# GLA recurrence followed by a multiplicative FFN: from the tenth step on, v's load is SyncE's first transfer of a step

## The chip, the cores and the metric

One core of a Trainium2 chip runs the kernel. Its engines are TensorE (PE in the profile, its weight loads PEld), VectorE (DVE), ScalarE (ACT), GpSimd (POOL) and SyncE (SP). Each works through its own instructions in order; they wait for one another through semaphores. SyncE computes nothing: it issues most of the transfers between HBM and the core's memory, one after another, into one queue that 16 DMA engines serve. The metric is the device time of one execution in microseconds, the median of the runs, lower is better.

## What is computed

The first part is a gated linear recurrence over 768 time steps for 4 batches and 8 heads of 48 values; its output, seen as 3072 tokens of 384 values, goes through a multiplicative FFN:

```python
# q, k, v, alpha: (4, 8, 768, 48), float32
for t in range(S):
    state = alpha[:, :, t, :, None] * state + np.einsum('bhd,bhe->bhde', k[:, :, t], v[:, :, t])
    y[:, :, t] = np.einsum('bhd,bhde->bhe', q[:, :, t], state)
x = y.transpose(0, 2, 1, 3).reshape(3072, 384)
a = x @ w1          # 384 x 1024
b = x @ w2          # 384 x 1024
h = a * b @ w3      # 1024 x 1024
out = h @ w_out     # 1024 x 384
```

The FFN's weights come in as 64-bit floats and are turned into float32 by integer and float operations on the chip.

## The kernel before

**Tiling.** Time is cut into chunks of 128 steps: 6 to a batch, 24 in all (N). A step of the main loop, n = 0 to 24, works on one chunk with all its heads, and on its neighbours, because the work is pipelined over the steps. Three chunks (384 tokens) make a group of the FFN; there are 8 groups. The kernel has two parts. In the first, the recurrence and the conversion of w1 and w2 run, and from step 6 on pieces of the FFN's first products (`gate`) fill TensorE's time. In the second, from about 188 us on, TensorE does the rest of the gates, the folding of w3 and w_out, and the last projection without a pause.

**A step of the first part, for n from 9 on.** In the order of the program:
- SyncE: `store()` writes chunk n-2's output x to the scratch tensor xd (four transfers, L307); in steps 11, 15 and 19 `load_x` reads a whole group of xd back as xT (L542); `load_a(n + 5)` loads alpha, `load_kq(n + 4)` loads k and q (L154, L155), and `load_v(n + 2)` loads v (L160). Transfers of raw weights (L238) and of gate results (`abd`, L631) stand between these blocks, where the program makes them.
- `attention(n)`: TensorE forms the scores of chunk n and, between them, the output of chunk n-1 (`quarters(n - 1)`, L426 and L466), which reads v(n-1) and a copy of it with the halves exchanged, vt. `transposed(n + 1)` turns q and k of the next chunk (L383), and ScalarE copies them out of PSUM (L385).
- `turn_v(n)`: GpSimd makes vt(n) from v(n) (L168, two instructions).
- the output of chunk n-1 is copied by ScalarE (L446); its stores go out in the next step.
- `outer(n)`: TensorE multiplies k and v of chunk n for the state (L395); chunks 11, 17 and 23 end a batch and need none.
- pieces of a gate (L556, nine products each): `exact` takes two PSUM banks. ScalarE moves the first to t (L565), VectorE adds the second to it (L567). Step 14 has two pieces here and one more later.
- `decayed(n + 2)`: VectorE multiplies q and k by the decays (L361). `logs(n + 4)`: ScalarE takes the logarithm of alpha (L326). `decays(n + 3)`: TensorE sums the logarithms over time (L348), ScalarE exponentiates (L351, L352).
- in some steps GpSimd carries the state's decay over a pair of chunks through small transfers: `ends` (L333, L354, L356) out and `dec` (L369) back, then L412 to L414.

**What sets the order.** Every engine's instructions stay close to the order of the program text; some are held behind marks (`tc.issue_after`). SyncE issues in order, too. So a load's place among SyncE's transfers is decided by where its call stands in the loop.

**Buffers.** v has four buffers (`vs`), so v(n+2) overwrites v(n-2). kq has three, alpha two, vt two. PSUM's eight banks are handed out in turn by `bank()`: the ninth request gets the first bank again and waits until that is read. Alpha of chunk n+5 is loaded in step n and read by ScalarE in step n+1; v of chunk n+2 is loaded in step n and used in steps n+2 and n+3; k and q of chunk n+4 are loaded in step n and read in step n+2.

`FIRST` is 6 and `TURNED` is 8.

Of the kernel before, what the change touches and what calls it, by code (L numbers as in the profile page):

```python
# [48 lines left out]
def kernel(  # L49
# [31 lines left out]
    TURNED = 8  # L81
# [30 lines left out]
    def after_marks(*names):  # L112
        stack = ExitStack()
        for x in names:
            stack.enter_context(tc.issue_after(mark[x]))
        return stack
# [15 lines left out]
    def rows(src, n):  # L132
        b, c = divmod(n, NCH)
        return src[b, :, ds(c * C, C), :].rearrange("h p d -> p h d")
# [4 lines left out]
    def load_a(n):  # L139
        if paired(n):  # L140
            if n % 2 == 0:
                b, c = divmod(n, NCH)
                x = pairs[n // 2 % 2]
                nc.sync.dma_start(out=x.rearrange("p h s d -> p h (s d)"), in_=alpha[b, :, ds(c * C, 2 * C), :].rearrange("h (p s) d -> p h (s d)", s=2))
                st["a", n] = st["a", n + 1] = x
        elif n < N:
            st["a", n] = inp.tile([C, H, D], FP32, tag="ac", name="ac", bufs=2)
            nc.sync.dma_start(out=st["a", n], in_=rows(alpha, n))

    def load_kq(n):  # L150
        if n >= N:
            return
        st["kq", n] = inp.tile([C, 2, H, D], FP32, tag="kq", name="kq")
        nc.sync.dma_start(out=st["kq", n][:, 0], in_=rows(k, n))  # L154
        nc.sync.dma_start(out=st["kq", n][:, 1], in_=rows(q, n))  # L155

    def load_v(n):
        if n < N:
            st["v", n] = vs[n % len(vs)]
            (nc.gpsimd if 2 < n < 8 else nc.sync).dma_start(out=st["v", n][:, :, 0:D], in_=rows(v, n))  # L160
# [121 lines left out]
    def fetch(ahead=3):  # L282
        while weights and len(begun) < ahead:
            begun.append(weights.popleft())
            next(begun[-1])
# [17 lines left out]
    def store():  # L303

        while later:
            dst, src = later.popleft()
            nc.sync.dma_start(out=dst, in_=src)  # L307
# [170 lines left out]
    def attention(n):  # L478

        low, high = quarters(n - 1) if turned(n - 1) else ([], [])  # L480
        done = None
        if n < N:
            own, done = quarter_scores(n)
            high = own + high
        low, high, at = deque(low), deque(high), [0, 0]
        while low or high:
            k = 0 if not high or low and at[0] <= at[1] else 1
            cost, f, x = (low, high)[k].popleft()
            at[k] += cost
            f(x)  # L490
        if done:
            done()

    def scores(n):
        qkT = st["qkT", n]
        sc = [bank().rearrange("p (j c) -> p j c", j=NP) for _ in range(2)]
        for j in range(NP):
            for i in range(2):
                r = ds(DP * i, D)
                nc.tensor.matmul(sc[i][:, j, :], qkT[r, 0, j, :], qkT[r, 1, j, :], start=True, stop=True)  # L500
        ms = work.tile([C, 2, NP, C], FP32, tag="ms", name="ms")
        for i in range(2):
            masked = nc.vector.tensor_tensor(ms[:, i].bitcast(I32), sc[i].bitcast(I32), keep_bc, op=ALU.bitwise_and)
        ends_of_part1[0] = mark["ms", n] = masked.ins
        st["ms", n] = ms
# [3 lines left out]
    def attend_state(n):  # L509
        qkT = st.pop(("qkT", n))  # L510

        y = [bank()[:, 0:HP * C].rearrange("p (j c) -> p j c", c=C) for _ in range(2)]
        st["y", n] = y, [(half * HP + j, i, y[i][ds(DP * half, DP), j, :])
                         for j in range(HP) for i in range(2) for half in range(2)]
        if n % NCH:
            for j, i, to in st["y", n][1]:
                r = ds(DP * i, D)
                nc.tensor.matmul(to, Ts[n % 2][r, j, :], qkT[r, 1, j, :],  # L520
                                 start=(j % HP == 0), stop=False, skip_group_check=True)
# [18 lines left out]
    def load_x(g, queue=nc.sync):  # L540
        st["xT", g] = xp.tile([C, KM, TG], FP32, tag="xT", name="xT")
        queue.dma_start(out=st["xT", g], in_=xd[g].rearrange("(k p) t -> p k t", p=C))  # L542
# [82 lines left out]
    def gate(g, f):  # L625
        yield from (late_gate if late else early_gate)(g, f)
# [68 lines left out]
    def run(pieces):  # L695

        for _ in range(pieces):
            if not fill:
                return
            try:  # L700
                next(fill[0])
            except StopIteration:
                fill.popleft()
# [22 lines left out]
    FIRST = 6  # L726
    begin = {FIRST - 3 + 4 * g: (g, range(FH if g < 4 else KF)) for g in range(5)}
    loads = {8: 1, 11: 2, 15: 3, 19: 4}

    for n in range(N + 1):  # L730
        if not 1 < n < FIRST:
            store()
        if n in loads:
            load_x(loads[n])
        if n != 1 and not 2 < n <= FIRST:
            load_a(n + 5)
        raws = (3, 3, 3, 3, 2, 2, 3, 3)[n] if n < 8 else 4
        for m in (n + 3,) * (n <= FIRST) + (n + 4,) * (n >= FIRST):
            load_kq(m)
            if 2 < n <= FIRST and m == n + 3:  # L740
                load_a(n + 5)
            if 1 < n < FIRST:
                store()
            if n < FIRST - 2:
                fetch(raws)
        if n >= FIRST:
            load_v(n + 2)
        if 0 < n <= TURNED:
            attend_state(n - 1)
        if n < TURNED:  # L750
            scores(n)
        else:
            attention(n)
        transposed(n + 1)
        if n == 1:
            decays(3)
            load_a(6)
            with after_marks(("e", 3)):
                logs(4)
        if n == FIRST + 1:  # L760
            run(2)
        if n < FIRST:
            with after_marks("pool"):
                load_v(n + 2)
        if n - 2 in begin and n > FIRST:
            g, tiles = begin[n - 2]
            with after_marks(("ms", n), ("qkT", n + 1)):
                split_x(g, 0)
            fill.extend(gate(g, f) for f in tiles)
        if n == FIRST:  # L770
            with after_marks("l", ("qkT", n + 1)):
                split_x(0, 0)
            fill.extend(gate(0, f) for f in begin[n - 3][1])
        pieces = ((3, 3, 2, 0) if n > FIRST + 3 else (0, 3, 3, 0))[(n - FIRST) % 4] if n >= FIRST else 0
        if n == 0:
            with after_marks(("qkT", 0)):
                logs(2)
            decays(2)
            with after_marks(("e", 2)):
                logs(3)  # L780
        early, ready = n < FIRST, len(thirds) if n > 2 else n // 2
        marks = (*[("qkT", n + 1)] * (n < N - 1), *[("qk", n + 1), ("ms", n)] * early, *["x3"] * (n - 2 in begin and n > FIRST))
        if n < N - 2 and n != FIRST:
            with after_marks(*marks):
                convert(2 if early else 1, raws)
        advance(n)
        turn_v(n)
        if n > TURNED:
            st.pop(("x", n - 1))()
        elif n:  # L790
            attend(n - 1)
        outer(n)
        if n > FIRST:
            third(ready)
        run(pieces > 0)
        if early:
            with after_marks(*marks):
                convert(1, raws)
        with after_marks(*[("ms", n)] * (n < 3)):
            decayed(n + 2)  # L800
        if not early:
            with after_marks(*[("qkT", n + 1)] * (n < N - 4)):
                logs(n + 4)
        if n == 4:
            load_x(0)
        convert(early and n > 0, raws)
        run(pieces > 1)
        if n:
            decays(n + 3)
        if n <= FIRST:  # L810
            third(ready)
        if 0 < n < FIRST:
            with after_marks(("e", n + 3)):
                logs(n + 4)
        if n == FIRST:
            with after_marks("x3", ("e", n + 3)):
                convert(2, raws)
        elif n < N - 2:
            convert(n == FIRST - 1 if early else n % 3 == 0, raws)
        if n == FIRST - 1:  # L820
            assert len(done) == 2 * KM
        run(pieces > 2)
        if n == N - 3:
            while begun:
                convert(1)
            weights.extend(load_out(j) for j in range(KF))
            fetch(4)
# [90 lines left out]
```

## Time and profile before

| | |
|---|---|
| median of 3 runs | 468.36 us (467.34 to 472.93) |
| the profiled execution | 467.49 us, span 465.8 us, mean granted TensorE clock 0.992 |
| TensorE busy | 448.6 us, 96% of the span |
| TensorE weight loads busy | 426.8 us, 92% |
| VectorE, ScalarE, GpSimd busy | 363.3 us (78%), 277.9 us (60%), 96.0 us (21%) |
| transfers | 80.38 MB, mean 173 GB/s; 97904 of 149381 packets under 512 B |
| v, issue to landing | 3.2 to 6.7 us, median 5.1 |
| alpha, issue to landing | 2.4 to 8.1 us, median 4.4 |
| k and q, issue to landing | 3.6 to 7.5 us, median 5.2 |

Of the page's view of 40 slices (11.6 us each), three rows: TensorE's busy tenths, the clock granted to it, and the load of the DMA engines:

```profile
PE   4998999997999999999999999999999999999996
PEclk9999999998899999999999999999999999999999
DMA  9999999987998878578755437412115976555511
```

The first part covers the first 16 slices. TensorE is busy nearly all the time after the first slice, with a dent in the tenth, where the clock is below full as well; the DMA engines are full for most of the first part and have room in the second.

### The profile page before, as it was taken

What the parts mean: (1) busy time and instruction counts of PE and PEld (TensorE: products, weight loads), DVE (VectorE), ACT (ScalarE), POOL (GpSimd) and SP (SyncE); (2) the same over time, 40 slices, a digit from 0 to 9 for tenths busy, and PEclk for the clock granted to TensorE, in tenths of its full rate; (3) what the DMA queues carried; (4) which work ended last, traced back from release to release, by engine and by line L of the source; (5) the groups of instructions that cost most, each with busy time, mean ns of one, the idle gap of its engine ahead of it and who ended that gap; (6) DMA issues with size and microseconds to landing.
All of it is one profiled execution on the core that took longest, in us unless ns stands there. A gap on an engine that the chain in (4) does not pass through costs nothing.

```text
span 465.8 us, 11170 instructions
## 1 busy us (share of the span) xinstructions
PE 448.6 (96%) x4296; PEld 426.8 (92%) x4296; DVE 363.3 (78%) x578; ACT 277.9 (60%) x544; POOL 96.0 (21%) x186
## 2 busy tenths in 40 slices
PE   4998999997999999999999999999999999999996
PEld 2676699986999999999999999999999999999996
DVE  2779995998578969999997899998542967766671
ACT  4685966866468554898765676765544533333330
POOL 6144323215222533022222111211110000000000
PEclk9999999998899999999999999999999999999999
DMA  9999999987998878578755437412115976555511
GB/s 175 257 207 223 269 220 219 225 190 187 184 189 169 181 161 220 178 233 235 212 183 185 132 125 193 146 48 91 51 35 144 243 223 182 184 171 161 168 51 52
DMA packets 149381, 80.38 MB, mean 173 GB/s; under 512 B 97904, under 2 KB 139120, under 8 KB 149328
## 3 DMA queue, kind: packets, MB, share of 16 engines
q1 hardware_dynamic: 143552, 64.44, 57.3%
q0 software_dynamic: 5776, 15.22, 11.1%
q8 instruction: 34, 0.56, 0.6%
q14 instruction: 19, 0.16, 0.1%
HBM read 57.58 MB, written 22.06 MB: 171 GB/s over the span
## 4 chain that ended last, share of the span: by engine, by line
PE 86%; DMA 5%; DVE 3%; ACT 3%; SPq 2%; issue 1%; DVEq 0%; ACTq 0%
PE bank L556 71%; PE bank L426 4%; PE bank L383 2%; PE bank L395 2%; DMA kq<-in_q_dram 2%; PE bank L466 2%; DMA v<-in_v_dram 1%; PE bank L500 1%; PE bank L345 1%; PE bank L342 1%; DMA raw<-in_moe_w_dram 1%; SPq L155 1%; DVE qk L361 1%; PE bank L348 1%; PE bank L526 1%
## 5 line engine op out<-in xcount | busy, mean ns | idle before, releaser
L556 PE MATMUL bank<-x,w 128*128 128x384 f32 x1152 | 211.1, 339 | 0.6 <-DVE ms L473 0.6
L556 PEld LDWEIGHTS bank<-x,w 128*128 128x128 f32 x1152 | 202.3, 189 | 1.9 <-DVE ms L473 1.0
L556 PE MATMUL bank<-w3o,ab 128*128 128x384 f32 x576 | 100.2, 336 | 0.0
L556 PEld LDWEIGHTS bank<-w3o,ab 128*128 128x128 f32 x576 | 99.9, 188 | 0.0
L581 ACT ACTIVATE bank<-bank 128x384 f32<-128x384 f32 x96 | 45.8, 477 | 40.4 <-PE bank L556 40.3
L565 ACT ACTIVATE t<-bank 128x384 f32<-128x384 f32 x64 | 31.6, 495 | 57.6 <-PE bank L556 57.6
L631 POOL DMA_DIRECT2D abd<-ab x45 | 25.8, 573 | 133.9 <-DVE ab L617 115.8
L682 DVE TENSOR_TENSOR ab<-abl,ab 128x1024 fp32r<-128x1024 f32 x24 | 29.4, 1224 | 12.8 <-ACT ab L681 12.7
L681 ACT ACTIVATE ab<-abl 128x1024 fp32r<-128x1024 f32 x24 | 25.5, 1061 | 20.1 <-PE bank L556 18.5
L556 PE MATMUL bank<-wo,w3T 128*128 128x384 f32 x192 | 35.9, 334 | 0.0
L617 DVE TENSOR_TENSOR ab<-bank,r 128x384 f32<-128x384 f32 x44 | 24.3, 552 | 13.6 <-ACT bank L581 7.0
L251 ACT ACTIVATE power<-power,rebias 128x512 uint32<-128x512 uint32 (+1 forms) x36 | 25.2, 701 | 14.1 <-DVE power L250 14.1
L556 PEld LDWEIGHTS bank<-wo,w3T 128*128 128x128 f32 x192 | 33.5, 188 | 0.0
L385 ACT COPY qkT<-bank 128x512 f32<-128x512 f32 x48 | 26.2, 599 | 10.2 <-PE bank L383 10.2
L361 DVE TENSOR_TENSOR qk<-kq,e 128x768 f32<-128x768 f32 x24 | 23.4, 976 | 10.9 <-ACT e L352 8.1
L567 DVE SCALAR_TENSOR_TENSOR o<-bank,t 128x384 f32<-128x384 f32 x24 | 13.4, 557 | 22.4 <-issue 13.7
L567 DVE SCALAR_TENSOR_TENSOR r<-bank,t 128x384 f32<-128x384 f32 x40 | 22.0, 551 | 10.7 <-ACT t L565 5.1
L683 DVE SCALAR_TENSOR_TENSOR ab<-ab,abl 128x1024 fp32r<-128x1024 f32 x24 | 29.2, 1218 | 0.0
L254 DVE SCALAR_TENSOR_TENSOR power<-raw,power 128x512 uint32<-128x512 uint32 (+1 forms) x36 | 23.9, 663 | 4.0 <-ACT power L251 4.0
L253 DVE SCALAR_TENSOR_TENSOR mant<-mant,rest 128x512 f32<-128x512 uint32 (+1 forms) x36 | 23.7, 658 | 2.5 <-ACT rest L246 2.5
L466 PE MATMUL bank<-qkT 48*64 48x128 f32 (+1 forms) x512 | 24.9, 247 | 0.0
L426 PE MATMUL bank<-ms,v 64*64 64x64 f32 (+1 forms) x256 | 24.4, 244 | 0.0
(100 smaller groups left out, 695.6 us busy)
## 6 DMA issues: line engine op xcount, KB each, us to landing
abl<-abd SPq DMA_DIRECT2D x24, 512.0 KB, 4.6
abd<-ab POOLq DMA_DIRECT2D x45, 192.0 KB, 3.0
raw<-in_moe_w_dram SPq DMA_DIRECT2D x64, 128.0 KB, 3.4
raw<-in_moe_w_dram SPq DMA_DIRECT2D x12, 512.0 KB, 5.9
xT<-xd POOLq DMA_DIRECT2D x9, 576.0 KB, 5.0
kq<-in_k_dram SPq DMA_DIRECT2D x24, 192.0 KB, 5.2
kq<-in_q_dram SPq DMA_DIRECT2D x24, 192.0 KB, 5.6
out_dram<-o SPq DMA_DIRECT2D x24, 192.0 KB, 3.5
```

Of the source, the lines that this page charges most:

```text
L361: mark["qk", n] = nc.vector.tensor_mul(qks[n % 3][:, :, :, 0:D], st.pop(("kq", n)), st.pop(("e", n)).rearrange("p i (h d) -> p i h d", h=H ...
L385: mark["qkT", n] = nc.scalar.copy(qkT[:, :, :, ds(DP * half, DP)], tp[half]).ins
L426: nc.tensor.matmul(to, w, x, start=(at, i) not in first, stop=True, skip_group_check=True)
L466: nc.tensor.matmul(sc[1][to, j, :] if late else sc[0][to, :, j, :], qkT[r, 0, j, ds(DP * late, DP)], q, start=True, stop=True)
L556: nc.tensor.matmul(p, w[part][i], x[part][i], start=start and part == parts[0] and i == 0, stop=stop and part == parts[-1] and i == n - 1, ...
L565: nc.scalar.activation(t, p1, AF.Copy, scale=(1.0 + 1.0 / P) * scale)
L567: nc.vector.scalar_tensor_tensor(to, p2, scale, t, op0=ALU.mult, op1=ALU.add)
L581: nc.scalar.activation(p, p, AF.Copy, scale=1.0 + 1.0 / P)
L631: (nc.gpsimd if late else nc.sync).dma_start(out=abd[g][:, f, :], in_=ab)
L681: nc.scalar.activation(t[:, 0], ab, AF.Copy, scale=1.0 - 2.0 ** -13)
L682: nc.vector.tensor_sub(t[:, 1], ab, t[:, 0].bitcast(FP32))
L683: nc.vector.scalar_tensor_tensor(t[:, 2], t[:, 0].bitcast(FP32), -1.0 - 1.0 / P, ab, op0=ALU.mult, op1=ALU.add)
```

## The change

From step 9 on (`n > TURNED`) the call of `load_v(n + 2)` stands at the top of the step, ahead of `store()`, `load_x`, `load_a` and `load_kq`, instead of behind them. For steps 6 to 8 it stays where it was. It concerns the loads of v(11) to v(23), made in steps 9 to 21; later calls do nothing.

```diff
     for n in range(N + 1):
+        if n > TURNED:
+            load_v(n + 2)
         if not 1 < n < FIRST:
             store()
         if n in loads:
...
                 store()
             if n < FIRST - 2:
                 fetch(raws)
-        if n >= FIRST:
+        if FIRST <= n <= TURNED:
             load_v(n + 2)
```

In the built kernel the order of instructions on TensorE, VectorE and ScalarE is the same as before. On SyncE the 13 loads of v stand ahead of their step's stores. On GpSimd two places change, although the text of the program does not: one of the two copies of v(11) (L168) now comes before the small store of alpha's row (L333), and the copies of v(15) come before two small loads (L369).

## Prediction

> **What bounds the kernel now.** The page's chain comes first: who sets the end.
>
> ```profile
> PE 86%; DMA 5%; DVE 3%; ACT 3%; SPq 2%; issue 1%; DVEq 0%; ACTq 0%
> ```
>
> TensorE does, so the change is worth what it adds to or takes from TensorE's idle time and slow time. The change touches steps 9 to 21, so I asked next for TensorE's waits from 56 to 190 us (total, times, longest):
>
> ```profile
> PE bank L395 <- DMA v<-in_v_dram: 3.3, 1, 3.3
> PE bank L556 <- DVE ms L473: 0.6, 1, 0.6
> ```
>
> One wait in the whole stretch is for v. TensorE's timeline shows it (start, time, engine, line, count, idle before); the last three lines are the same work a step later, undisturbed:
>
> ```profile
> 115.01 1.10 PE L395 MATMUL bank<-v,qk 128*64 128x48 f32 x16 [3.33 <-DMA v<-in_v_dram]
> 116.03 5.39 PE L556 MATMUL bank<-x,w 128*128 128x384 f32 x18
> ...
> 125.97 0.67 PE L395 MATMUL bank<-v,qk 128*64 128x48 f32 x16
> 126.57 3.41 PE L556 MATMUL bank<-x,w 128*128 128x384 f32 x18
> 129.81 0.51 PE L348 MATMUL bank<-la,sums 128*128 128x384 f32 x2
> ```
>
> This is outer(14), in step 14: TensorE was ready at 115.01 - 3.33 = 111.68. And what follows the wait is slow: 1.10 us for 0.67, and 5.39 for 3.41. The granted clock (PEclk, ahead of the last two columns) says why:
>
> ```profile
> 113.00:113.50 0.50, 0.00 (x0) 0.00 (x0) 0.50 (x2) 0.50 (x2) 0.10 (x1) 1.00 0.63 230
> 113.50:114.00 0.50, 0.00 (x0) 0.00 (x0) 0.50 (x3) 0.14 (x1) 0.00 (x0) 0.56 0.99 373
> 120.00:120.50 0.50, 0.50 (x3) 0.50 (x3) 0.00 (x0) 0.00 (x0) 0.50 (x1) 0.62 1.29 204
> 120.50:121.00 0.50, 0.50 (x5) 0.50 (x4) 0.00 (x0) 0.07 (x1) 0.50 (x2) 1.00 0.87 206
> ```
>
> It halves at about 113.56 (0.56 over that half microsecond is 0.06 us at full and 0.44 at half), 1.9 us after TensorE stopped, and is full again at about 120.38. Last, SyncE's own order in step 12, which loads v(14), and the next alpha:
>
> ```profile
> 104.28 1.87 SPq L307 DMA_DIRECT2D xd<-x  x4
> 106.25 0.40 SPq L148 DMA_DIRECT2D ac<-in_alpha_dram  x1
> 106.69 0.58 SPq L154 DMA_DIRECT2D kq<-in_k_dram  x1
> 107.32 1.90 SPq L155 DMA_DIRECT2D kq<-in_q_dram  x1
> 109.33 0.81 SPq L160 DMA_DIRECT2D v<-in_v_dram  x1
> ...
> 115.10 0.40 SPq L148 DMA_DIRECT2D ac<-in_alpha_dram  x1
> ```
>
> v(14) is issued last, at 109.33, and lands 5.6 us later, at 114.97.
>
> **Part 1: v goes to the front (13 loads, v(11) to v(23)).** No instruction is added or removed. In step 12 v would be issued where the first store now stands, at 104.28, 5.05 us sooner. The v loads of this profile took 3.2 to 6.7 us to land, median 5.1; so it lands at 107.5 to 111.0, by the median at 109.4, all before 111.68. The wait of 3.33 goes, and with it the slow clock: 1.10 - 0.67 = 0.43 and 5.39 - 3.41 = 1.98. Sum: 5.74 us. Other v loads that are close get slack too: v(18), issued at 139.49, lands 5.3 later at 144.8, and TensorE uses it at 145.41.
>
> Does v wait longer at the front? It overwrites the buffer of v(n-2), whose last readers are GpSimd's copies in step n-2 and the quarters of attention(n-1). The stores behind it send ScalarE's copy of those same quarters, which comes later. So whatever holds v would have held the stores; v(14)'s buffer was last read at 91.3 (the end of attention(11)), 13 us before. I cost this wait at nothing. If the cover were gone, the four stores, alpha, k and q behind v would be held by as much.
>
> **Part 2: what v passes is issued later.** Per step these are four output stores, alpha, k and q, and in steps 11, 15 and 19 the load of xT. Each is later by one issue of v (0.40 to 0.81 us where it isn't held) and at most by one transfer of v: k and q, the same 192 KB, land 0.7 to 1.1 us apart in this stretch. It doesn't add up over the steps, since a step still sends the same bytes: each is one v behind, once. Lower bound: nothing or a gain, because from 103.6 to 107.6 the DMA engines were about half idle (share 0.62, after 1.26 in the 3.6 us before) and v would fill that. Upper bound 0.81 + 1.05 = 1.9 us. I take 0 for alpha(18), nearest to the row where the queue had a hole.
>
> [...]
>
> **Part 3: what is late next.** Alpha. Its lead is a single step, and ScalarE, which works in order, takes its logarithm ahead of clearing the gate's banks:
>
> ```profile
> 118.29 0.52 ACT L326 ACTIVATE la<-ac 128x384 f32<-128x384 f32 x1 [4.64 <-DMA ac<-in_alpha_dram]
> 118.72 0.47 ACT L565 ACTIVATE t<-bank 128x384 f32<-128x384 f32 x1
> 119.39 0.56 DVE L567 SCALAR_TENSOR_TENSOR r<-bank,t 128x384 f32<-128x384 f32 x1 [1.69 <-PE bank L556]
> ```
>
> ScalarE waited 4.64 us for alpha(18) and nobody noticed, since TensorE stood still for v. Without that, TensorE goes from 111.68 through outer(14), 18 + 9 gate products and decays(17). A step later this took 131.81 - 125.97 = 5.84, so attention(15) is due at 117.5. The eight banks go round in turn: step 14 takes 14 (2 sums, 2 scores, 2 transposes, 1 outer, 2 + 2 + 2 for the gate, 1 decays), so attention(15)'s second sum takes the bank that this t clears, and its first score bank the one that this r clears, at 119.39 + 0.56 = 119.95. TensorE then idles from 117.5 to 119.9: 2.4 us come back. With alpha(18) later by 0 to 1.9 this is 2.4 to 4.3; if it landed 2.4 sooner, 0.
>
> Does the clock halve again? In the trace it did after 1.9 us of idle time and didn't after the 0.63 us at 94.56 (clock 1.00 there). 2.4 lies above the first, so I can't exclude it: bounds 0 and the 0.43 + 1.98 = 2.41 us measured; I take a third, 0.8, since this gap is the shorter one. [...]
>
> Alpha(22) is next in line (landed 4.5 us after 144.59, at 149.1; ScalarE waited 0.7 us for it). With TensorE 2.5 us earlier, attention(19), now at 151.3, is due at 148.8, while the second t behind that alpha ends at 149.54 + 0.48 = 150.0: up to 1.2 us come back. But SyncE was held there by the queue (1.19 us at 140.23, 2.96 for four stores at 141.52) behind v(18), which is now gone sooner. I take 0 and keep 1.2 for the range. k and q have over 2 us (k(20) and q(20) landed by 142.8 and are read at 149.48).
>
> GpSimd's queue changes in two places. The copies of v(11) come partly in front of the store of alpha's row (now at 85.86): v(11), at 79.05 instead of 84.83, should land by 84.2. The copies of v(15) come in front of two small loads (now at 120.00): v(15), from 111.38, lands by about 116.5. Nothing, while v is that early.
>
> Sum: -5.74 + 2.4 + 0.8 = -2.5 us. The profiled execution took 467.49 us (span 465.8, 1.7 around it), 0.87 below the median of the runs, 468.36; so 465.0 for it, and 465.9 for the median.
>
> **The rivals.** *Full gain:* alpha(18) lands before 116 too because v left the hole earlier and the queue is shorter, and nothing comes back: 468.36 - 5.74 = 462.6. For it: that half idle stretch. Against: from 107.6 to 115 the share was 0.86, and alpha(18) stays behind as many bytes. *A wait in place of another:* alpha(18) lands about 0.9 later, TensorE stands 3.3 us at attention(15) and the clock halves: 3.3 + 2.4 = 5.7, so 468.4, no change. *Slower:* one mechanism, alpha behind v in the queue at attention(15). From a landing 0.9 us later than now on, the new gap costs more than the old; at the full 1.9 the gap is 4.3 + 2.4 = 6.7, +1.0 net; held once more by a full queue, as SyncE was for 2.54 us at 101.18, the gap is 6.8 + 2.4, +3.5. So 469.4 to 471.9, say 470.7. For it: alpha(17) (issued at 106.25, landed 4.2 later) came just as ScalarE read it, at 110.44, so alpha has no slack here. *The move doesn't happen* is out: the instruction order of the built kernel shows all 13 loads ahead of their stores.
>
> **How the numbers follow.** Partial gain 0.50 (own range 464 to 467.5), full gain 0.18, no change 0.17, slower 0.15. The range 462.2 to 470.6 takes in the first three and half the last. Two per cent, 9.4 us, is about what a measurement of this kernel tells from no change. Faster than 459.0 would need more idle time than steps 9 to 24 hold (5.74 + 0.63): 0.02. Slower than 477.7 needs several new gaps with a halved clock: 0.06. Within: 0.92.
>
> **What would show it.** The 3.33 us wait of L395 for v is gone, and the 18 products behind it take 3.4 us. TensorE has a gap at attention(15) (L426, L466), released by ScalarE's t or VectorE's r behind an alpha; its length against 2.4 us decides between the cases, and the clock rows whether it halved. Wrong if v is still waited for, if SyncE is held at L160 by TensorE or GpSimd, or if step 15 has no gap (full gain).

## The result and the profile after

| | before | after |
|---|---|---|
| median of 22 runs each, on the same chip | 467.32 us (465.31 to 472.93) | 464.66 us (462.91 to 467.82) |
| ratio, 95% interval | | 0.9946 [0.9928, 0.9965] |
| the profiled execution | 467.49 us, span 465.8 us | 467.82 us, span 466.1 us |

The change is worth about 2.5 us (0.54% of 467.3), well inside two per cent. The profiled execution of the changed kernel is the slowest of its 22, slower than the profiled one before: stages have to be compared, not spans. TensorE reached the transposes (L383) of step 9, where the change begins, 1.17 us later than before (80.12 instead of 78.95), although nothing was changed up to there. From there to the transposes of step 22 it took 92.63 us instead of 93.58.

TensorE's waits from 56 to 190 us (total, times, longest), the changed kernel:

```profile
PE bank L466 <- ACT t L565: 2.2, 1, 2.2
PE bank L556 <- DVE ms L473: 0.7, 1, 0.7
```

The wait of L395 for v, 3.3 us, is gone; a wait for ScalarE's t of 2.2 us is there. TensorE's timeline in steps 14 and 15 (start, time, engine, line, count, idle before):

```profile
113.45 0.67 PE L395 MATMUL bank<-v,qk 128*64 128x48 f32 x16
114.05 3.41 PE L556 MATMUL bank<-x,w 128*128 128x384 f32 x18
...
119.30 0.43 PE L426 MATMUL bank<-qkT,T 48*64 48x128 f32 x4
121.96 0.48 PE L466 MATMUL bank<-qkT 48*64 48x128 f32 x2 [2.23 <-ACT t L565]
```

outer(14) goes through at full speed: 0.67 us instead of 1.10, and 3.41 instead of 5.39 for the 18 products behind it. Then attention(15) stops for 2.23 us. What released it, in ScalarE's timeline:

```profile
121.01 0.52 ACT L326 ACTIVATE la<-ac 128x384 f32<-128x384 f32 x1 [5.62 <-DMA ac<-in_alpha_dram]
121.44 0.85 ACT L565 ACTIVATE t<-bank 128x384 f32<-128x384 f32 x2
```

ScalarE stood 5.62 us in front of the logarithm, for alpha(18), and the t that clears a bank of PSUM came behind it. The granted clock (third column from the right) around this gap:

```profile
121.00:121.50 0.50, 0.00 (x0) 0.00 (x0) 0.00 (x0) 0.49 (x2) 0.50 (x2) 1.00 1.11 222
121.50:122.00 0.50, 0.04 (x4) 0.04 (x4) 0.06 (x1) 0.50 (x3) 0.50 (x1) 0.64 0.80 159
...
125.00:125.50 0.50, 0.50 (x18) 0.47 (x10) 0.50 (x2) 0.10 (x1) 0.20 (x1) 0.95 1.19 240
```

It halves at 121.64 and is full again at 125.05, 3.41 us later. Before, the slow stretch was 6.83 us long. Last, SyncE's order in steps 12 and 13:

```profile
106.11 0.38 SPq L160 DMA_DIRECT2D v<-in_v_dram  x1
106.58 2.09 SPq L307 DMA_DIRECT2D xd<-x  x4
108.77 0.40 SPq L148 DMA_DIRECT2D ac<-in_alpha_dram  x1
...
112.83 0.38 SPq L160 DMA_DIRECT2D v<-in_v_dram  x1
113.31 3.33 SPq L307 DMA_DIRECT2D xd<-x  x4
116.75 0.40 SPq L148 DMA_DIRECT2D ac<-in_alpha_dram  x1
```

v(14), issued at 106.11, lands at 109.78, 3.7 us ahead of its use. Alpha(18), in step 13, goes out behind v(15) and four stores that hold SyncE for 3.33 us, and lands at 120.98.

The balance can be checked term by term. From the transposes of step 14 to those of step 15 TensorE took 14.36 us before (110.96 to 125.32) and 12.75 after (112.80 to 125.55): 1.61 less. The terms are -5.74 (the wait and the slow clock at outer(14)), +2.23 (the gap) and +1.97 (attention(15) needed 6.25 - 2.23 = 4.02 us of work to the transposes, where before it needed 125.32 - 123.27 = 2.05), together -1.54.

### The profile page after: what moved, and what is told of

Its sections match the earlier page's. It is cut to its first block, busy times and chain, and to the rows that moved or that the text cites. A ratio compares the mean times of both kernels' runs of the same rounds, so it can differ in the third digit from the quotient of the medians.

```text
span 466.1 us, 11166 instructions
## 1 busy us (share of the span) xinstructions
PE 448.6 (96%) x4296; PEld 425.3 (91%) x4296; DVE 362.8 (78%) x578; ACT 277.4 (60%) x544; POOL 96.0 (21%) x186
## 4 chain that ended last, share of the span: by engine, by line
PE 84%; DMA 6%; DVE 3%; ACT 3%; issue 1%; SPq 1%; DVEq 0%; ACTq 0%
PE bank L556 70%; PE bank L426 4%; DMA kq<-in_q_dram 3%; PE bank L383 2%; PE bank L466 2%; DMA ac<-in_alpha_dram 2%; PE bank L395 1%; DVE qk L361 1%; PE bank L342 1%; PE bank L345 1%; DMA kq<-in_k_dram 1%; PE bank L348 1%; PE bank L500 1%; PE bank L526 1%; DMA abd<-ab 1%
## 5 line engine op out<-in xcount | busy, mean ns | idle before, releaser
L556 PEld LDWEIGHTS bank<-x,w 128*128 128x128 f32 x1152 | 200.1, 188 | 2.8 <-DVE ms L473 1.3
L466 PE MATMUL bank<-qkT 48*64 48x128 f32 (+1 forms) x512 | 26.3, 254 | 2.2 <-ACT t L565 2.2
L466 PEld LDWEIGHTS bank<-qkT 48*64 48x64 f32 x512 | 23.8, 139 | 2.8 <-ACT t L565 2.5
```

The source lines that it names most:

```text
L466: nc.tensor.matmul(sc[1][to, j, :] if late else sc[0][to, :, j, :], qkT[r, 0, j, ds(DP * late, DP)], q, start=True, stop=True)
L556: nc.tensor.matmul(p, w[part][i], x[part][i], start=start and part == parts[0] and i == 0, stop=stop and part == parts[-1] and i == n - 1, ...
```

## The experiments

The time from the transposes of step 9 to those of step 22 is cut at steps 12 and 15. These are the starts of L383 on TensorE in the profiled executions, and the waits are TensorE's in that stretch. "v" are waits for v, "alpha" waits that a late alpha causes through ScalarE (t or e), "q" those through VectorE's decayed q and k (r), "none" idle time without a releaser in the profile, always at attention(10); "slow" counts stretches of 3.41 us at half clock. Waits for VectorE's masked scores (ms, up to 0.78 us in seven of the executions) are left out. Each row is one profiled execution, and the experiments are told below.

| kernel | steps 9 to 12 | 12 to 15 | 15 to 22 | v | alpha | q | none | slow |
|---|---|---|---|---|---|---|---|---|
| before | 21.33 | 25.04 | 47.21 | 3.33 | | | | 2 |
| before, again | 21.95 | 21.28 | 50.02 | 0.67 + 1.89 | 0.52 | | | |
| before, log behind t | 22.01 | 23.69 | 47.80 | 2.83 + 0.52 | | | 0.43 | 1 |
| v(14) alone to the front | 21.36 | 20.17 | 49.54 | 1.52 | | | | |
| all but v(14) to the front | 21.81 | 20.48 | 47.30 | 0.45 | | | 0.89 | |
| after | 22.00 | 23.43 | 47.20 | | 2.23 | | | 1 |
| after, again | 23.70 | 19.30 | 47.26 | | | | 1.33 | 1 |
| alpha ahead of v | 22.12 | 19.48 | 48.95 | | | 1.01 | 1.31 | |
| alpha ahead of v, again | 21.81 | 20.86 | 48.94 | | 0.76 | 1.45 | | |
| stores ahead of v | 21.72 | 23.03 | 49.16 | | 1.23 + 1.58 + 0.93 + 0.53 | | 0.90 | |
| after, log behind t | 22.26 | 19.22 | 47.21 | | | | 1.44 | |
| after, log behind t, again | 23.69 | 19.30 | 48.28 | | 0.52 | | 1.32 | 1 |
| v(14) at the back, log behind t | 21.86 | 20.75 | 47.61 | 1.47 | | | 0.26 | |
| from v(13) on, log behind t | 23.88 | 19.30 | 47.21 | | | | 1.52 | 1 |

**One transfer alone, and all but that one.** The theory was that the wait of outer(14) carries the change. Against the changed kernel:

```diff
-        if n > TURNED:
+        if n == 12:
             load_v(n + 2)
...
-        if FIRST <= n <= TURNED:
+        if n >= FIRST and n != 12:
             load_v(n + 2)
```

> Only v(14) is loaded at the front of its step; the other twelve loads stay behind k and q as before. Theory A (one transfer, v(14), carried the gain): as the whole change, 2.7 us faster than before (ratio 0.992 to 0.997), no wait of L395 for v, and a gap of 1.5 to 2.5 us at attention(15) that ends with ScalarE's t behind alpha(18). Rival B (the gain is spread over thirteen loads and a queue with fewer holes): at most a third of it, ratio 0.998 or more.

465.84 us, ratio 0.9971 [0.9947, 0.9996]: by the medians a little over half of the gain, which neither side had expected (the interval takes in the whole gain and almost none). The wait for v did not vanish but moved on to step 18, where v(18) is still SyncE's last transfer (the waits of TensorE in this kernel, then the instruction that waited):

```profile
PE bank L395 <- DMA v<-in_v_dram: 1.5, 1, 1.5
```

```profile
142.63 0.46 PE L395 MATMUL bank<-v,qk 128*64 128x48 f32 x9 [1.52 <-DMA v<-in_v_dram]
```

The other half of the pair leaves v(14) where it was and moves the 12 others, again against the changed kernel:

```diff
-        if n > TURNED:
+        if n > TURNED and n != 12:
             load_v(n + 2)
...
-        if FIRST <= n <= TURNED:
+        if FIRST <= n <= TURNED or n == 12:
             load_v(n + 2)
```

> The complement: twelve loads of v at the front, v(14) behind k and q as before. Theory A: no gain, ratio 0.998 to 1.003, and TensorE still waits about 3 us for v at outer(14) with the clock halved after it. Rival B: two thirds of the gain or more, ratio 0.996 or less.

463.44 us, ratio 0.9923 [0.9897, 0.9948]. By the medians that is at least the whole gain, without the transfer that was thought to make it. The theory of the one transfer falls. v(14), last again, was waited for by 0.45 us only: it was issued 3.7 us ahead of the transposes of step 14, where before it was 1.6.

**The kernel before, and the changed one, in another execution.** Was the wait of step 14 the kernel's or that execution's?

> The kernel before, unchanged, traced a second time. Theory A' (the four loads of a step issued in a row hold SyncE and land late, so that v is late in some step of nearly every execution, though not always in step 14): again a wait of L395 for v of 1 us or more, in step 14 or in a step whose v had under 1 us of slack (18, 22), and v(14) issued within 1.5 us of 109.3 counted from the same point of TensorE's work. Rival E (the 3.3 us wait in the first trace was an accident of that execution): no wait of L395 for v over 0.5 us.

TensorE's waits, the kernel before:

```profile
PE bank L395 <- DMA v<-in_v_dram: 2.6, 2, 1.9
PE bank L466 <- ACT t L565: 0.5, 1, 0.5
```

Now it waited 0.67 us in step 14 and 1.89 in step 18. So the sum of the waits for v belongs to the kernel (3.33 and 2.56 us in the two executions, and 3.35 in the one with only the logarithm moved); the step in which they fall does not. v(14) was issued 3.2 us ahead of the transposes of step 14, 1.6 us sooner than in the first execution, where theory A' had at most 1.5.

> The changed kernel, unchanged, traced a second time. Theory A': no wait of L395 for v over 0.5 us in any step; at attention(15) a gap of 1 to 2.5 us behind alpha(18), or none if alpha(18) lands before TensorE gets there. Rival E: some wait for v over 1 us also here.

TensorE had no gap at attention(15) in this execution of the changed kernel. ScalarE still waited for alpha(18):

```profile
118.22 0.52 ACT L326 ACTIVATE la<-ac 128x384 f32<-128x384 f32 x1 [1.54 <-DMA ac<-in_alpha_dram]
```

but TensorE was not yet there, because it had lost time in step 10:

```profile
84.91 0.32 PE L426 MATMUL bank<-ms,vt 64*64 64x128 f32 x2 [1.33 <-issue]
```

After this gap the clock was half for 3.41 us. What was lost early was not lost again later: alpha(18) landed 4.1 us after the transposes of step 14, where in the other execution of this kernel it was 8.2. The gap at attention(15) follows from that distance. In the execution with the gap, TensorE was due 6.93 us after the transposes (119.73 - 112.80), and the bank was free 0.98 us after alpha landed (121.96 - 120.98). So the gap is the distance less 5.95, less what TensorE had already stood since the transposes. This was worked out from one execution; the eight others with the logarithm ahead of t agree with it. In five of them it gives no gap or almost none, and none behind t is there: the kernel before (7.31 - 5.95 - 3.33 is below zero), after, again (4.10), v(14) alone (6.11, which leaves 0.16), all but v(14) (6.41, which leaves 0.01 behind the wait of 0.45 for v) and the first execution with alpha ahead of v (5.42). For the kernel before, again, this gives 7.21 - 5.95 - 0.67 = 0.59, measured 0.52; for alpha ahead of v, again, 6.78 - 5.95 = 0.83, measured 0.76; for stores ahead of v 8.83 - 5.95 - 1.23 = 1.65, measured 1.58.

**Alpha ahead of v.** If alpha(18) is what is late next, it can go first, with v second and the stores, k and q behind.

```diff
         if n > TURNED:
+            load_a(n + 5)
             load_v(n + 2)
...
-        if n != 1 and not 2 < n <= FIRST:
+        if n != 1 and not 2 < n <= FIRST and n <= TURNED:
             load_a(n + 5)
```

> From step 9 on alpha's load goes first, then v, then stores, k, q. Theory A (what came back after the change came through alpha(18) in SyncE's queue): alpha(18) is issued 3 us or more sooner against TensorE, the gap at attention(15) shrinks from 2.2 us to under 0.7, the clock stays full there, and the time is 1.5 to 4 us below the changed kernel's, ratio to before 0.987 to 0.991. Rival C (the queue as a whole is the limit, so another transfer is late in alpha's place): a gap of 1.5 us or more for v, k or q, ratio 0.993 to 0.997.

466.98 us, ratio 0.9995 [0.9963, 1.0026]: the whole gain is given back, which neither theory had. A second execution was profiled, to see where:

> Alpha first, then v, traced a second time, to see what ate the gain that the first trace promised: over the steps 9 to 22 a gap of TensorE of 2 us or more in total outside attention(15), for GpSimd's copies, for k and q, or for instructions (no releaser), against under 1 us for the changed kernel in the same steps.

SyncE's order in step 13 there, VectorE's timeline around 122 us, and TensorE behind it:

```profile
112.37 0.86 SPq L160 DMA_DIRECT2D v<-in_v_dram  x1
113.28 4.84 SPq L307 DMA_DIRECT2D xd<-x  x4
118.16 0.44 SPq L154 DMA_DIRECT2D kq<-in_k_dram  x1
118.65 0.58 SPq L155 DMA_DIRECT2D kq<-in_q_dram  x1
```

```profile
122.59 0.96 DVE L361 TENSOR_TENSOR qk<-kq,e 128x768 f32<-128x768 f32 x1 [1.63 <-DMA kq<-in_q_dram]
123.47 0.55 DVE L567 SCALAR_TENSOR_TENSOR r<-bank,t 128x384 f32<-128x384 f32 x1
```

```profile
124.07 0.45 PE L556 MATMUL bank<-x,w 128*128 128x384 f32 x1 [1.45 <-DVE r L567]
```

Four stores hold SyncE for 4.84 us in front of k(17) and q(17). VectorE waits 1.63 us for q and starts its r only behind that, at 123.47, and TensorE waits 1.45 us for the bank that r clears. It is the same kind of wait as alpha's, one engine further. In the first of the two executions the waits were 1.19 and 1.01 us. Alpha(18) itself did go out sooner, 0.09 and 0.76 us after the transposes of step 14 where the first execution of the changed kernel had 3.95, but took 5.33 and 6.02 us to land instead of 4.23.

These waits do not account for the whole loss. From step 9 to step 22 the two executions took 90.55 and 91.61 us, less than the three with all of v at the back (93.25 to 93.58), and both were faster (465.34 and 465.20 us) than the median of this version. Where its slower runs lose the rest was not seen.

**The stores ahead of v.** Must v stand in front of the stores, or only in front of alpha, k and q?

```diff
-        if n > TURNED:
-            load_v(n + 2)
         if not 1 < n < FIRST:
             store()
         if n in loads:
             load_x(loads[n])
+        if n > TURNED:
+            load_v(n + 2)
         if n != 1 and not 2 < n <= FIRST:
```

> From step 9 on v's load stands behind the four stores (and load_x), still ahead of alpha, k and q. Theory A (what counts is that v is out of the back of the burst of alpha, k, q and v, not that it is first): v(14) and v(18) are not waited for or by under 0.6 us, alpha(18) is no later than in the changed kernel, ratio 0.992 to 0.996. Theory B (v must be in front of the stores, because the stores of 8-byte-by-8-byte scattered x hold SyncE and the queue): v is waited for again by more than 1 us in step 14 or 18, ratio 0.997 or above. By the traces of before, v would be issued some 2 us later than at the front and 3 us sooner than at the back, so it would land at about 112 in step 12, within 0.5 us of its use: I expect A, 0.994.

468.9 us, ratio 0.9999 [0.9974, 1.0024]. Both theories missed: v is never waited for (as A had it), and yet nothing is gained. (The stores write rows of 128 values, 512 bytes each, not pieces of 8 bytes as theory B has it.) Alpha is late, twice and more (ScalarE, then TensorE):

```profile
112.66 0.53 ACT L326 ACTIVATE la<-ac 128x384 f32<-128x384 f32 x1 [1.44 <-DMA ac<-in_alpha_dram]
...
120.71 0.52 ACT L326 ACTIVATE la<-ac 128x384 f32<-128x384 f32 x1 [4.85 <-DMA ac<-in_alpha_dram]
```

```profile
114.40 0.45 PE L556 MATMUL bank<-x,w 128*128 128x384 f32 x1 [1.23 <-ACT e L352]
```

The waits for alpha add up to 4.27 us in steps 14, 15, 18 and 19, more than those for v ever did. Alpha(18) landed 8.83 us after the transposes of step 14, against 8.18 and 4.10 in the two executions of the changed kernel. The same transfers stand ahead of alpha in both orders; why nothing is gained with the stores in front of v was not settled.

**The logarithm behind the first t.** The other way to take alpha off the path: let ScalarE clear the gate's first bank before it waits for alpha.

```diff
-        nc.scalar.activation(t, p1, AF.Copy, scale=(1.0 + 1.0 / P) * scale)
+        mark["t"] = nc.scalar.activation(t, p1, AF.Copy, scale=(1.0 + 1.0 / P) * scale).ins
...
-            with after_marks(*[("qkT", n + 1)] * (n < N - 4)):
+            with after_marks(*[("qkT", n + 1)] * (n < N - 4), *["t"] * (TURNED < n < N - 4 and pieces > 0)):
                 logs(n + 4)
```

> No transfer moves against the changed kernel; ScalarE takes alpha's logarithm one place later, behind the first t of the step's gate. Theory A (TensorE waited for a bank that ScalarE could not clear while it stood at alpha(18)): the gap at attention(15) goes from 2.2 us to under 0.5 with ScalarE still waiting some 4 us for alpha, clock full, ratio to before 0.987 to 0.991. Rival D (TensorE waited there for something else that came at the same time, such as the exponentials or q and k): the gap stays above 1.5 us, ratio 0.993 to 0.997.

462.91 us, ratio 0.9913 [0.9885, 0.9941]. ScalarE's timeline:

```profile
116.77 0.49 ACT L565 ACTIVATE t<-bank 128x384 f32<-128x384 f32 x1
118.78 0.53 ACT L326 ACTIVATE la<-ac 128x384 f32<-128x384 f32 x1 [1.52 <-DMA ac<-in_alpha_dram]
119.21 0.47 ACT L565 ACTIVATE t<-bank 128x384 f32<-128x384 f32 x1
```

The first t goes ahead of the logarithm; ScalarE waits for alpha(18) behind it, and no wait of TensorE is left from step 11 on. But this trace does not show that the move took a gap away. TensorE had stood 1.44 us at attention(10), and alpha(18) landed 4.59 us after the transposes of step 14. That is less than 5.95, so there would have been no gap with the logarithm first either. The same edit on the kernel before, where v is still late:

> The kernel before with one edit, the logarithm of alpha behind the first t of the step's gate; v stays behind k and q. Theory A (alpha matters only once v is early): TensorE still waits for v, ratio to before 0.997 to 1.003. Rival F (the place of the logarithm is a gain of its own): ratio 0.995 or less.

467.41 us, ratio 0.997 [0.9942, 0.9999], with waits for v of 2.83 and 0.52 us: while v is late, there is little for this edit to take. The two gains, 0.3% and 0.54%, about add up to the 0.87% of both; the intervals are too wide to say more.

> The same kernel as the run with the logarithm behind the first t, timed once more. Theory A (with the logarithm behind t a late alpha costs TensorE nothing, and this is worth more than the change alone): ratio 0.990 to 0.993, 462.5 to 464 us, and no gap at attention(15) released by t. Theory B (the first time was a lucky one, and what is left is the change's own 2.5 us): ratio 0.994 to 0.996, 464.5 to 466 us.

Timed once more, it gave 464.9 us, ratio 0.9923 [0.9897, 0.9949], with one gap of 0.52 us behind a t, at attention(19). Both intervals lie below one, so this version is faster than the kernel before. That it also beats the changed kernel (0.9946 [0.9928, 0.9965]) is not shown: both ratios lie lower, but the intervals overlap, and the traces do not decide. Here, too, alpha(18) came early, 5.20 us after the transposes of step 14. In none of the five profiled executions with the logarithm behind t was it late enough for the move to show at attention(15).

**Two combinations.** The first keeps v(14) at the back and has the logarithm behind t:

> Both of the best parts together: every v from v(11) at the front except v(14), and ScalarE's logarithm of alpha behind the first t of the step. Theory A (what is left after the change is the wait of ScalarE for alpha and the gap without a releaser in step 10): the logarithm's move has nothing left to do where no alpha is late, so the ratio is that of the better part, 0.991 to 0.993 (463 to 464 us). Theory B (the gains add): 0.987 to 0.990, 461.5 to 462.5 us.

464.82 us, ratio 0.9925 [0.9901, 0.995]: the gains do not add. v(14) was waited for by 1.47 us this time. The second moves v to the front from step 11 on only (`n > TURNED + 2`), with the logarithm behind t, and is about the idle time without a releaser:

> v goes to the front from step 11 on only (v(13) and later); v(11) and v(12) stay at the back of steps 9 and 10; the logarithm of alpha stands behind the first t. Theory A (the idle time of 0.9 to 1.4 us without a releaser at attention(10), seen only with v at the front, comes of v(11) or v(12) at the front): it is below 0.5 us here, as in the kernel before, and the time is 0.5 to 1.4 us below that of the run with the logarithm behind t: ratio 0.988 to 0.990. Theory B (that idle time is the moment's chance): it is as often there as not, and the ratio stays 0.991 to 0.993.

464.46 us, ratio 0.9921 [0.989, 0.9952], and TensorE in step 10:

```profile
84.18 0.32 PE L426 MATMUL bank<-ms,vt 64*64 64x128 f32 x2 [1.52 <-issue]
```

The gap is there with v(11) and v(12) at the back, so it does not need these loads at the front; the theory that it comes of them falls.

## Why the prediction was right

The forecast was a gain of 2.5 us; measured were 2.66 (467.32 to 464.66). The path that it names, a wait for v that goes and a smaller one behind alpha that comes, is what the first trace shows, and later executions bear it out. That the size fits so well is in part luck: it was added up from one execution, and several of its terms were off in ways that cancel.

- **Part 1, the wait for v: right, and more general than it was put.** The wait of 3.33 us and the slow clock of 2.41 us are gone, as worked out. But v(14) is not special. Waits for v of 2.56 to 3.35 us in sum are in all three executions with v at the back, in step 14, 18 or both, and in none of the eight in which every v from v(13) on stands ahead of k and q (among them the two with alpha first and the one with the stores first). That v(18) "gets slack" was said in passing; in one execution it was the larger part. In that execution the clock stayed full from step 9 on, so v cost 2.56 us there and not 5.74.
- **v itself waits for nothing new at the front: right.** The prediction called it a sign of being wrong if TensorE or GpSimd held SyncE at L160. By name they do, for 3.5 us in all of the changed profile, where before it was 4.4. The longest of these, 1.56 us, ends with GpSimd's copies (L168) of v(17), which do not read the buffer that v(18) takes, so it is not v's own buffer that is waited for. With v(14) at the back and the logarithm behind t, v(18) went out 0.18 us before those copies ended.
- **Part 2, what v passes is later by 0 to 1.9 us, taken as 0: inside the bounds, not at the value.** Against the transposes of step 14 alpha(18) landed 0.87 us later than before in the first trace (8.18 instead of 7.31 us). It was issued no later (3.95 instead of 4.14) but took 4.23 us to land instead of 3.17. In the other trace it landed 3.2 us sooner (4.10), after TensorE had stood in step 10. The bound was drawn for SyncE alone; the larger swing comes from where TensorE is.
- **Part 3, alpha next: the mechanism right, the size partly by luck.** The gap is at attention(15), released by t, behind the logarithm of alpha(18): 2.23 us against 2.4. With alpha 0.87 later the prediction's own working gives 3.3. Two of its terms made the gap too long: the stop ended with t, 0.98 us after alpha landed, and not with r, 1.68 us after it (119.95 - 118.27); and TensorE was due 6.93 us after the transposes, not 6.56 (117.52 - 110.96). Of the five executions with v from v(11) on in front and the logarithm ahead of t, the gap shows in three, 2.23, 0.76 and 1.58 us; in the two others alpha(18) landed less than 5.95 us after the transposes.
- **The clock: the term that was mis-sized.** Taken were 0.8 us, a third of 2.41, because the gap would be the shorter one; in the first trace it was 1.97, in others nothing. From step 9 on the slow clock came in whole stretches of 3.41 us, and the length of the gap alone did not decide; see below.
- **Alpha(22): nothing, as taken,** in both traces of the changed kernel. **GpSimd's two places: nothing**, as taken, though the loads were later than worked out: v(11) went out at 82.64 (79.05 expected) and landed at 88.04 (84.2 expected), v(15) landed at 119.53 (116.5 expected). TensorE waited for neither.
- **Not foreseen:** the idle time without a releaser at attention(10), 0.26 to 1.52 us in nine of the 14 executions.
- **The rivals.** A step 15 without a gap was to mean the full gain. The second trace of the changed kernel has no gap there, but its time went in step 10, and it ran at 464.93 us. No change is what the first trace suggests by its span. The slower case, alpha behind more transfers, is in part what the stores ahead of v show: 4.27 us of waits for alpha, and a ratio of 1. (Its 2.54 us at 101.18 are the length of one issue of SyncE, behind those of k, q and v; that a full queue held it is the prediction's reading of that time.)

Where does the rest of the wait go? Part into alpha's gap, part into step 10 and the slow clock behind it. From step 9 to step 22 the three executions with all of v at the back took 93.58, 93.25 and 93.50 us (mean 93.4), the two of the changed kernel 92.63 and 90.26 (91.4), those with the logarithm behind t as well 88.69 and 91.27 (90.0). The medians stand in the same order: 467.3, 464.7, and 462.9 to 464.9 us.

## What to carry to other kernels

When a transfer that is waited for moves to the front of a queue, list what it passes, find each one's first reader, and then what stands behind that reader on its engine: here a late alpha or q stopped TensorE only through the clearing of a PSUM bank queued behind it. Moving that one instruction ahead of the wait is worth a try, but here it was not shown to add to the gain. Moving the next transfer forward as well (alpha) gained nothing: q was late in its place. A wait in one trace is one sample; profile the same kernel twice before tying a gain to one instruction, and sum the waits by kind.

## What the runs showed of the hardware

**The clock changed on a grid.** In the first execution of either kernel all changes of the granted clock lie whole multiples of 3.413 us apart. In the kernel before its record begins, at full, at 17.98 (16 products of L395 at 16.66 still took 1.10 us, those of step 15 took 0.67), and it halved at 113.56, 95.58 us or 28 times later; in the changed one the record begins at 15.83 (the same products, at 16.30, took 0.67), and it halved at 121.64, 105.81 us or 31 times later. It was full again two such stretches later in the kernel before (120.38) and one later in the changed one (125.05). Counted over these stretches from step 9 on in all runs, the clock halved after each of the three in which TensorE had stood 1.88 us or more at full clock, after three of the seven with 1.32 to 1.68 us, and after none with 1.23 or less. The 1.89 us in step 18 of the kernel before, again, were cut by the grid into 1.68 and 0.21, and the clock stayed full; in its first execution it halved after 1.88 us within one stretch. What tells the three of the seven apart stayed open: all three are at attention(10), with its small products, but so is the gap of 1.44 us after which the clock stayed full. Idle time alone does not decide: ahead of step 9 the clock halved in four executions, after stretches with 0.70, 0.92, 1.32 and 1.36 us of it.

**A gap without a releaser.** In nine of the 14 executions TensorE stood at one and the same instruction in step 10, for 0.26 to 1.52 us, and went on 1.36 to 1.55 us after the end of a packet of 16 KB of the queue marked as instruction (q8 in the profile). In the runs with all but v(14), with the logarithm behind t, with v(13) on and with the logarithm behind t again, for example, the packet ended at 81.85, 85.02, 82.72 and 83.60 us, and TensorE went on 1.50, 1.52, 1.46 and 1.36 us later. In these nine the packet ended 2.57 to 3.93 us after the transposes of step 9. Four executions without the gap had it earlier, 1.55 to 1.94 us after them. That TensorE stands there until some time after this packet fits these 13. It does not fit the first execution of the kernel before: there the packet ended 2.61 us after the transposes, and TensorE went on 0.9 us later (82.44) without a gap. The profile does not say what the packet holds or for whom, either. So what TensorE waited for there was not shown, nor why the packet came when it did.
